# Router's successors in two scaled float16 parts instead of two float32r parts

## Chip, core and metric

The kernel runs on one core of a Trainium2 chip. The metric is device time in microseconds (us). The kernel before took 1172.93 us, the median of three runs (1170.28 to 1175.97).

## The reference, cut to what matters

Three stages follow each other. Attention gives 2304 tokens of 512 features; a router picks one of 8 experts for each token; a dense feed-forward layer follows for all tokens.

```python
attn = softmax(scale * mean_pairs(q) @ k.T)        # (4,8,576,1152), head size 64
x    = (attn @ v)                                  # 2304 tokens x 512
logits = x @ w_gate + modality_bias[modality_id]   # the router
e_idx, gate_w = argmax(logits), softmax(logits)[e_idx]
out[mask] = gate_w[mask] * (relu(x[mask] @ w1[e]) @ w2[e])    # w1: 512x1024, w2: 1024x512
h = out @ w_in                                     # 512x2048
y = (relu(h) + log1p(exp(-abs(h)))) @ w_out        # 2048x512
```

## The kernel before, in words

**Attention** (`attention`, up to about 508 us) keeps q and k in two float16 parts and makes router tables between its heads. The last of these steps stand in `lstage`; step `gb` adds 1e-9 to the softmax sum, `gc` inverts it, and `gd` multiplies the inverse into the scale `r` with which the tokens are written to `x_dram`.

**Experts** (`Moe`, `Early`). Tokens are sorted by expert into blocks of 256. `Early` works on one block while the last router tables are made. Then a loop in `moe_ffn` goes over nine blocks, called block 0 to 8 here. A block has 16 units: eight of `L1` (x @ w1, relu) and eight of `L2` (@ w2). Each unit needs one weight tile `mhl` [128,2,512], which `split` makes out of half of a raw tile `mraw`: ScalarE writes the rounded high part (L645), and VectorE, or GpSimd for splits 7 and 15 of a block, subtracts it to give the low part (L646). A raw tile comes by DMA from the SyncE queue (L633); there are four raw buffers and four `mhl` buffers. In blocks 1 to 7 the same four raw buffers also take 20 tiles of `w_in` and `w_out` (`convert`, L984 to L987: a float64 is turned into a float32), three per block and two in block 7. `split` inside `moe_ffn` (L731, L733) makes high and low parts of these.

Every product is three matmuls (`three`, L608 to L610: high x high, high x low, low x high); the same three stand in `F2` (L779 to L781).

**Feed-forward** (`Ffn`, from about 762 us). `F1` is x @ w_in with the softplus in pieces on ScalarE and VectorE; `F2` is @ w_out, seven units behind. Tokens go in groups of 256 or 512, so a matmul has 256 or 512 columns in `F1` and 512 in `F2`.

The parts are float32r tiles. TensorE and SyncE follow the order of the code in the second half; the order of the other engines is made by the tile framework.

Of the kernel before, what the change touches and what calls it, by code (L numbers as in the profile page):

```python
# [9 lines left out]
F32=mybir.dt.float32; F32R=mybir.dt.float32r; F16=mybir.dt.float16; I32=mybir.dt.int32; U32=mybir.dt.uint32  # L10
ACTF=mybir.ActivationFunctionType; ALU=mybir.AluOpType; AX=mybir.AxisListType
# [5 lines left out]
def attention(ctx,late,tc,I,C,x_dram,LG,gate,fill,early):  # L17

    nc=tc.nc
# [197 lines left out]
    def lstage(b,half,last=False):  # L217

        z={}
# [10 lines left out]
        V=nc.vector  # L230
# [391 lines left out]
class Moe:  # L622
# [16 lines left out]
    def split(s):  # L639
        n=s.nsplit  # L640
        if n>=16: return
        s.nsplit+=1
        t=s.P['hl'].tile([128,2,512],F32R,name="mhl")
        r=s.raw[n//2][:,n%2]
        s.nc.scalar.copy(out=t[:,0],in_=r)  # L645
        (s.nc.gpsimd if n%8==7 else s.nc.vector).tensor_tensor(out=t[:,1],in0=r,in1=t[:,0].bitcast(F32),op=ALU.subtract)  # L646
        s.hl[n]=t
    def advance(s):
        s.split()
# [3 lines left out]
        for _ in range(m): s.split()  # L653
    def T(s,h):
        def f():
            if h==0: s.x=s.P['x'].tile([128,4,2,TB],F32R,name="xx")
            X=s.tr()
            for k in range(4): s.nc.tensor.transpose(X[:,k],s.xg[h][:,128*k:128*k+128],s.K.ident)
            cs=slice(128*h,128*h+128)
            s.nc.scalar.copy(out=s.x[:,:,0,cs],in_=X)  # L660
            s.nc.vector.tensor_tensor(out=s.x[:,:,1,cs],in0=X,in1=s.x[:,:,0,cs].bitcast(F32),op=ALU.subtract)
        return f
    def L1(s,i):
        def f():
            if i==0: s.h=s.P['h'].tile([128,8,2,TB],F32R,name="hT")
            if i%2==0: s.l=s.lt()
            w=s.hl.pop(i)
            for k in range(4):
                s.K.three(s.l[:,i%2],w[:,0,128*k:128*k+128],w[:,1,128*k:128*k+128],(s.x[:,k,0],s.x[:,k,1]),k==0,k==3)
            if i%2:  # L670
                l,z=s.l,slice(i-1,i+1)
                s.nc.scalar.activation(out=s.h[:,z,0],in_=l,func=ACTF.Relu)
                s.nc.vector.scalar_tensor_tensor(out=s.h[:,z,1],in0=l,scalar=0.0,in1=s.h[:,z,0].bitcast(F32),op0=ALU.max,op1=ALU.subtract)
            s.advance()
        return f
    def L2(s,d,half):
# [12 lines left out]
class Early(Moe):  # L689
# [18 lines left out]
        for h in range(2): at(279+3*h,s.T(h))  # L708
    def done(s,d,y):
        yy=s.P['ye'].tile([128,2,TB],F32,name="ye")  # L710
        s.nc.scalar.copy(out=yy,in_=y)
        s.K.lag(2,lambda: s.nc.sync.dma_start(out=s.YE[d//2],in_=yy))
    def step(s,n=1):
        for _ in range(n):
# [2 lines left out]
def moe_ffn(ctx,mst,tc,I,C,Y,YE,wsp,W32,out,convert,ncv,K,P,bl):  # L717
# [3 lines left out]
    nc=tc.nc  # L721
    ident=C['ident']; IDX,IDS,EV,OFF,CIDS=C['IDX'],C['IDS'],C['EV'],C['OFF'],C['CIDS']
    SP=[mybir.EngineType.SP]
    wip=ctx.enter_context(tc.tile_pool(name="wip",bufs=1,reuse_waits="tile"))
    WIH=wip.tile([128,4,DF],F32R,name="WIH"); WOH=wip.tile([128,16,DM],F32R,name="WOH")
    WL=[None]*32
    unit,lag,flush,three,reg=K.unit,K.lag,K.flush,K.three,K.reg
    def split(i):

        h=WIH[:,i%4,512*(i//4):512*(i//4)+512] if i<16 else WOH[:,i-16]  # L730
        nc.scalar.copy(out=h,in_=W32[i])  # L731
        WL[i]=wsp.tile([128,512],F32R,name=f"wl_{i}",tag=f"ws{i}")
        nc.vector.tensor_tensor(out=WL[i],in0=W32[i],in1=h.bitcast(F32),op=ALU.subtract)  # L733
    def WIL(k,f0): return WL[4*(f0//512)+k][:,f0%512:f0%512+128]
    def WOL(fc): return WL[16+fc]
    class Ffn:

        def __init__(s,n,x2,scat,P): s.n=n; s.x2=x2; s.scat=scat; s.P=P; s.g={}; s.m={}; s.e={}; s.hh={}; s.c=4//n; s.nu=16//s.c
        def F1(s,u,ks=range(4)):

            def f():
                q,t=divmod(u,2); c=s.c
                if ks[0]==0:
                    s.hh[u]=(P['pt'].tile([128,4,128],F32,name="tr") if u>=4 and len(ks)==2 else s.P['pl'].tile([128,2,TB],F32,name="l")).rearrange("p a b -> p (a b)").rearrange("p (a b) -> p a b",a=c)
                h=s.hh[u]
                for i in range(c):
                    f0=128*(c*u+i)
                    for k in ks:
                        three(h[:,i],WIH[:,k,f0:f0+128],WIL(k,f0),s.x2(k),k==0 and (i==0 or len(ks)==4),k==3 and (i==c-1 or len(ks)==4))
                if ks[-1]!=3: return  # L750
                if t==0: s.m[q]=s.P['tmp'].tile([128,2,512],F32,name="m"); s.e[q]=s.P['tmp'].tile([128,2,512],F32,name="e")
                hh=h.rearrange("p a b -> p (a b)")
                nc.scalar.activation(out=s.e[q][:,t],in_=hh,func=ACTF.Abs)  # L753
                nc.vector.tensor_scalar(out=s.m[q][:,t],in0=hh,scalar1=0.0,scalar2=None,op0=ALU.max)  # L754
                if t==1:
                    m,e=s.m.pop(q),s.e.pop(q)
                    nc.scalar.activation(out=e,in_=e,func=ACTF.Exp,scale=-1.0)
                    nc.vector.tensor_tensor(out=m,in0=m,in1=e,op=ALU.add)
                    nc.vector.tensor_scalar(out=e,in0=e,scalar1=1.0,scalar2=None,op0=ALU.add)
                    nc.vector.scalar_tensor_tensor(out=m,in0=e,scalar=1.0,in1=m,op0=ALU.subtract,op1=ALU.subtract)  # L760
                    def b():
                        nc.scalar.activation(out=e,in_=e,func=ACTF.Ln)  # L762
                        for i in range(2):
                            nc.vector.tensor_tensor(out=m[:,i],in0=e[:,i],in1=m[:,i],op=ALU.subtract)
                            g=s.P['g'].tile([128,2,512],F32R,name="g"); s.g[2*q+i]=g
                            nc.scalar.copy(out=g[:,0],in_=m[:,i])
                            nc.vector.tensor_tensor(out=g[:,1],in0=m[:,i],in1=g[:,0].bitcast(F32),op=ALU.subtract)
                    lag(BLAG,b)
            return f
        def F2(s,u,ks=None):  # L770
            def f():
                ks_=range(s.n) if ks is None else ks
                if u==0: s.o=[s.P['po'].tile([128,DM],F32,name=f"o{k}") for k in range(s.n)]
                g=s.g[u].rearrange("p s (i w) -> p s i w",i=s.c)
                for i in range(s.c):
                    fc=s.c*u+i
                    for k in ks_:
                        cs=slice(128*k,128*k+128); o=s.o[k]
                        nc.tensor.matmul(o,lhsT=g[:,0,i,cs],rhs=WOH[:,fc],start=(fc==0),stop=False)  # L779
                        nc.tensor.matmul(o,lhsT=g[:,0,i,cs],rhs=WOL(fc),start=False,stop=False)  # L780
                        nc.tensor.matmul(o,lhsT=g[:,1,i,cs],rhs=WOH[:,fc],start=False,stop=(fc==15))  # L781
                if u==s.nu-1:
                    for k in ks_:
                        ob=s.P['io'].tile([128,DM],F32,name="io")
                        if k%2: nc.vector.tensor_copy(out=ob,in_=s.o[k])
                        else: nc.scalar.copy(out=ob,in_=s.o[k])  # L786
                        ap,lim=s.scat(k)
                        nc.gpsimd.indirect_dma_start(out=out,out_offset=bass.IndirectOffsetOnAxis(ap=ap.bitcast(U32),axis=0),in_=ob,in_offset=None,bounds_check=2303,oob_is_err=False)  # L788
            return f
# [5 lines left out]
    XH={}; YR={}; PF=dict(yr=P['raw'])  # L795
# [84 lines left out]
    with tc.For_i(0,nrem,1):  # L880
        with ExitStack() as st:
# [162 lines left out]
```

## Time and profile before

| what | value |
|---|---|
| median of three runs | 1172.93 us |
| the profiled execution's own time | 1169.95 us |
| its span, first to last instruction | 1168.1 us |
| mean granted TensorE clock | 0.997 of full speed |
| TensorE busy (PE) | 1120.9 us, 96%, 7887 instructions |
| weight loads (PEld) | 829.3 us, 71% |
| VectorE (DVE) | 865.9 us, 74% |
| ScalarE (ACT) | 641.3 us, 55% |
| GpSimd (POOL) | 468.5 us, 40% |

A busy TensorE is not one at its peak, since matmuls overlap and their ends are modelled: the pace is read from the distance between the starts of two matmuls. The idle time named in a row is that of the engine before the instruction, with what ended it.

### The profile page before, as it was taken

To read this page: it belongs to the slowest core of one execution; us is meant where nothing else is said; L and a number is where in the kernel's file an instruction comes from. 1 tells how busy PE (TensorE), PEld (TensorE's weight loads), DVE (VectorE), ACT (ScalarE), POOL (GpSimd) and SP (SyncE) were. 2 spreads that over 40 slices of the span, in tenths; PEclk is the share of its full clock that TensorE was granted. 3 is DMA by queue.
4 is the path that set the end of the run, shared out by engine and by line. 5 is a ranking of instruction groups with operands and counts; after the bars stand their busy time and mean duration, and the time that the engine had idled before them with its cause. 6 is when DMAs were issued, how large, how long until landed. Compare 5 with 4: busy or idle time off the path is not lost. (4 is left out here: it accounts for less than half of the span.)

```text
span 1168.1 us, 20814 instructions
## 1 busy us (share of the span) xinstructions
PE 1120.9 (96%) x7887; PEld 829.3 (71%) x7887; DVE 865.9 (74%) x1583; ACT 641.3 (55%) x1096; POOL 468.5 (40%) x512
## 2 busy tenths in 40 slices
PE   5899999999999999999999999999999999999996
PEld 2444555455545555579999999998888888889995
DVE  5778798769876888689798878659667666766662
ACT  5666656766667655647555666555444444444440
POOL 6888877898788866722221121100000100100100
PEclk9999999999999999999999999999999999999998
DMA  9334436341743151436778887531000000000000
GB/s 240 83 83 108 118 89 179 99 118 59 193 115 109 35 145 39 164 94 217 238 249 281 284 272 272 187 90 43 19 1 27 36 5 14 37 5 6 37 10 30
DMA packets 42939, 129.47 MB, mean 111 GB/s; under 512 B 5841, under 2 KB 12881, under 8 KB 40914
## 3 DMA queue, kind: packets, MB, share of 16 engines
q1 hardware_dynamic: 39794, 118.12, 33.9%
q0 software_dynamic: 3040, 9.96, 2.5%
q8 instruction: 65, 1.06, 0.4%
q14 instruction: 40, 0.33, 0.1%
HBM read 108.13 MB, written 20.45 MB: 110 GB/s over the span
## 5 line engine op out<-in xcount | busy, mean ns | idle before, releaser
L121 DVE TENSOR_REDUCE mx<-sr 128x1 f32<-128x384 f32 x432 | 225.4, 549 | 93.0 <-PE sr L117 74.1
L172 ACT ACTIVATE P<-st 128x576 f32<-128x576 f32 x288 | 186.1, 651 | 153.6 <-PE st L169 142.1
L186 POOL TENSOR_TENSOR acc<-P 128x288 f32<-128x288 f32 x192 | 160.2, 856 | 84.4 <-ACT P L172 80.7
L212 PE MATMUL pv<-P,v 128*64 128x288 f32 x1152 | 174.3, 419 | 0.3 <-ACT P L172 0.3
L788 POOL DMA_INDIRECT out_dram<-io,CIDS x18 | 18.7, 1039 | 383.2 <-ACT io L786 335.5
L169 PE MATMUL st<-Q,KB 128*128 128x288 f16 x576 | 153.3, 287 | 2.4 <-ACT Q L152 2.4
L168 PE MATMUL st<-Q,KA 128*128 128x288 f16 x576 | 155.2, 290 | 0.0
L186 POOL TENSOR_TENSOR acc<-acc,P 128x288 f32<-128x288 f32 x176 | 147.7, 860 | 8.5 <-ACT P L172 6.9
L117 PE MATMUL sr<-KA,Q 128*128 128x384 f16 x384 | 113.2, 334 | 17.9 <-DVE mx L121 9.1
L609 PE MATMUL l<-xf,WIH 128*128 128x256 f32 (+1 forms) x384 | 129.1, 336 | 0.1
L608 PE MATMUL l<-xf,WIH 128*128 128x256 f32 (+1 forms) x384 | 129.0, 336 | 0.0
L610 PE MATMUL l<-xf,wl 128*128 128x256 f32 (+1 forms) x384 | 129.0, 336 | 0.0
L645 ACT CAST mhl<-mraw 128x512 fp32r<-128x512 f32 x160 | 97.0, 618 | 54.7 <-PE l L610 22.2
L212 PEld LDWEIGHTS pv<-P,v 128*64 128x64 f32 x1152 | 70.3, 136 | 73.6 <-issue 35.6
L646 DVE TENSOR_TENSOR mhl<-mraw,mhl 128x512 fp32r<-128x512 f32 x140 | 96.3, 707 | 32.9 <-ACT mhl L645 32.4
L168 PEld LDWEIGHTS <-KA 128*128 128x128 f16 x576 | 56.3, 98 | 86.0 <-issue 76.0
L779 PE MATMUL o<-WOH,g 128*128 128x512 f32 x288 | 112.3, 390 | 0.0
L780 PE MATMUL o<-wl,g 128*128 128x512 f32 x288 | 112.2, 390 | 0.0
L781 PE MATMUL o<-WOH,g 128*128 128x512 f32 x288 | 112.0, 389 | 0.0
L762 ACT ACTIVATE e<-e 128x1024 f32<-128x1024 f32 x36 | 38.2, 1060 | 100.3 <-DVE m L760 100.3
L754 DVE TENSOR_SCALAR m<-l 128x512 f32<-128x512 f32 x72 | 49.4, 687 | 57.1 <-ACT e L753 57.0
L94 POOL TENSOR_TENSOR KB<-kr,KA 64x576 f16<-64x576 f32 x64 | 83.6, 1311 | 4.6 <-ACT KA L90 2.4
(260 smaller groups left out, 2543.0 us busy)
## 6 DMA issues: line engine op xcount, KB each, us to landing
mraw<-in_wm_dram SPq DMA_DIRECT2D x80, 512.0 KB, 4.6
kr<-in_k_dram SPq DMA_DIRECT2D x30, 576.0 KB, 9.5
qr<-in_q_dram SPq DMA_DIRECT2D x16, 576.0 KB, 6.5
v<-in_v_dram SPq DMA_DIRECT2D x16, 576.0 KB, 4.4
mraw<-in_w_out_dram SPq DMA_DIRECT2D x16, 512.0 KB, 4.4
stg<-in_w_in_dram SPq DMA_DIRECT2D x12, 512.0 KB, 6.2
y_dram<-w SPq DMA_DIRECT2D x20, 256.0 KB, 4.4
xs_dram<-xs SPq DMA_DIRECT2D x24, 192.0 KB, 2.1
```

Source lines behind the costliest of these rows:

```text
L117: nc.tensor.matmul(sr[:,:KW],lhsT=q[:,h,0,r0:r0+128],rhs=ka[:,h,k0:k0+KW],start=True,stop=True)
L121: nc.vector.tensor_reduce(out=MX[p][:,t,kh:kh+1],in_=sr[:,:KW],axis=AX.X,op=ALU.max,negate=True)
L168: nc.tensor.matmul(st[:,h,:HQ],lhsT=ka[:,h,ks],rhs=q[:,h,0,qs],start=True,stop=False)
L169: nc.tensor.matmul(st[:,h,:HQ],lhsT=kb[:,h,ks],rhs=q[:,h,1,qs],start=False,stop=True)
L172: nc.scalar.activation(out=P[g],in_=ST.pop(g)[:,:,:HQ],func=ACTF.Exp,scale=1.0/16)
L186: for h in range(2): nc.gpsimd.tensor_tensor(out=A[:,h],in0=B_[:,h],in1=P[g][:,h],op=ALU.add)
L212: nc.tensor.matmul(t[64*h:64*h+64,:HQ],lhsT=V[p][:,c,64*h:64*h+64],rhs=P[g][:,h],start=(c==0),stop=(c==NCH-1))
L608: nc.tensor.matmul(o,lhsT=wh_,rhs=x[0],start=first,stop=False)
L609: nc.tensor.matmul(o,lhsT=wh_,rhs=x[1],start=False,stop=False)
L610: nc.tensor.matmul(o,lhsT=wl_,rhs=x[0],start=False,stop=last)
L779: nc.tensor.matmul(o,lhsT=g[:,0,i,cs],rhs=WOH[:,fc],start=(fc==0),stop=False)
L780: nc.tensor.matmul(o,lhsT=g[:,0,i,cs],rhs=WOL(fc),start=False,stop=False)
```

## The change

High and low parts of weights and activations behind the router become float16. Before rounding, weights are scaled by a power of two (SW for the experts, SI and SO for the two feed-forward weights) and tokens by SX, which enters through the router's gate; results are scaled back where PSUM is read. Attention keeps its own order of two chunks and its formats. The edits by kind:

```diff
-            V.tensor_scalar(out=g,in0=g,scalar1=1e-9,scalar2=None,op0=ALU.add)
+            V.tensor_scalar(out=g,in0=g,scalar1=1e-9,scalar2=1.0/SX,op0=ALU.add,op1=ALU.mult)
+SX=16.0; SW=16.0; SI=16.0; SO=256.0
...
-        t=s.P['hl'].tile([128,2,512],F32R,name="mhl")
+        t=s.P['hl'].tile([128,2,512],F16,name="mhl")
         r=s.raw[n//2][:,n%2]
-        s.nc.scalar.copy(out=t[:,0],in_=r)
-        (s.nc.gpsimd if n%8==7 else s.nc.vector).tensor_tensor(out=t[:,1],in0=r,in1=t[:,0].bitcast(F32),op=ALU.subtract)
+        s.nc.scalar.activation(out=t[:,0],in_=r,func=ACTF.Copy,scale=SW)
+        if n%8==7:
+            s.nc.gpsimd.tensor_scalar(out=r,in0=r,scalar1=SW,scalar2=None,op0=ALU.mult)
+            s.nc.gpsimd.tensor_tensor(out=t[:,1],in0=r,in1=t[:,0],op=ALU.subtract)
+        else:
+            s.nc.vector.scalar_tensor_tensor(out=t[:,1],in0=r,scalar=SW,in1=t[:,0],op0=ALU.mult,op1=ALU.subtract)
...
-        s.nc.scalar.copy(out=yy,in_=y)
+        s.nc.scalar.activation(out=yy,in_=y,func=ACTF.Copy,scale=1.0/(SW*SW))
...
-                        if k%2: nc.vector.tensor_copy(out=ob,in_=s.o[k])
-                        else: nc.scalar.copy(out=ob,in_=s.o[k])
+                        if k%2: nc.vector.tensor_scalar(out=ob,in0=s.o[k],scalar1=1.0/SO,scalar2=None,op0=ALU.mult)
+                        else: nc.scalar.activation(out=ob,in_=s.o[k],func=ACTF.Copy,scale=1.0/SO)
```

The same is done to the tiles `x`, `h`, `WIH`, `WOH`, `WL`, `g` and `xf`, to `split` in `moe_ffn`, and to the reads of PSUM in `F1` (Abs with a scale, max with a factor). The code now begins eight lines lower, so L608 to L610 become L611 to L613, L645 becomes L648, and L646 becomes L650 to L653.

On TensorE, at the first unit of a block (l is the result in PSUM, xx the tokens, mhl the weights), before:

```order
L608 MATMUL l_7182<-xx_7059,mhl_7096 128x256
L609 MATMUL l_7182<-xx_7059,mhl_7096 128x256
L610 MATMUL l_7182<-xx_7059,mhl_7096 128x256
L608 MATMUL l_7182<-xx_7059,mhl_7096 128x256
L609 MATMUL l_7182<-xx_7059,mhl_7096 128x256
```

and now:

```order
L611 LDWEIGHTS mhl_7098
L611 MATMUL l_7184<-xx_7061,mhl_7098 128x256
L612 LDWEIGHTS mhl_7098
L612 MATMUL l_7184<-xx_7061,mhl_7098 128x256
L613 LDWEIGHTS mhl_7098
L613 MATMUL l_7184<-xx_7061,mhl_7098 128x256
```

Each float16 matmul has an instruction of its own that loads its weights; a float32r matmul brings them itself. The sequence of products is the same.

On GpSimd, in the block loop (io are gathered tokens, mraw the raw weights), before:

```order
L637 DMA io_7177<-xs_dram_62,IDX_102 128x512
L646 TENSOR_TENSOR mhl_7266<-mraw_7118,mhl_7266 128x512
L637 DMA io_7360<-xs_dram_62,IDX_102 128x512
L637 DMA io_7403<-xs_dram_62,IDX_102 128x512
L646 TENSOR_TENSOR mhl_7420<-mraw_7269,mhl_7420 128x512
```

and now:

```order
L640 DMA io_7179<-xs_dram_62,IDX_102 128x512
L650 TENSOR_SCALAR mraw_7120<-mraw_7120 128x512
L651 TENSOR_TENSOR mhl_7268<-mraw_7120,mhl_7268 128x512
L640 DMA io_7363<-xs_dram_62,IDX_102 128x512
L640 DMA io_7406<-xs_dram_62,IDX_102 128x512
L650 TENSOR_SCALAR mraw_7272<-mraw_7272 128x512
L651 TENSOR_TENSOR mhl_7423<-mraw_7272,mhl_7423 128x512
```

A product with SW, written back into the raw tile, now stands ahead of each subtraction on GpSimd. On VectorE, ScalarE and SyncE no instruction changes its place; only forms and line numbers differ.

## Rows read from the trace of the kernel before

**Rows 1.** Stages, blocks: window us; length, busy PE, PEld, DVE, ACT, POOL; clock; DMA
```profile
508.40:540.70 32.30, 29.41 (x296) 27.99 (x292) 27.70 (x86) 19.75 (x38) 9.35 (x8) 1.00 0.49 158
...
564.70:589.05 24.35, 24.19 (x202) 23.99 (x201) 19.82 (x31) 15.15 (x27) 4.61 (x4) 1.00 0.80 271
589.05:616.20 27.15, 25.82 (x226) 25.08 (x225) 24.78 (x52) 15.07 (x27) 6.12 (x4) 1.00 0.77 256
...
665.20:690.60 25.40, 24.51 (x202) 24.07 (x201) 20.74 (x33) 14.98 (x27) 5.72 (x4) 1.00 0.80 265
...
739.20:762.40 23.20, 23.20 (x196) 23.20 (x195) 11.36 (x17) 12.31 (x24) 2.59 (x2) 1.00 0.50 165
762.40:1158.80 396.40, 396.31 (x2016) 339.08 (x2015) 265.79 (x355) 173.46 (x249) 17.71 (x17) 1.00 0.08 25
```

**Rows 2.** Timeline, TensorE, blocks 6 and 7: start us, us, engine, line, op, tiles
```profile
709.38 0.28 PE L608 MATMUL l<-hT,mhl 128*128 128x256 f32 x1
...
718.26 0.28 PE L610 MATMUL l<-xx,mhl 128*128 128x256 f32 x1
```

**Rows 3.** Timeline, TensorE, the last units of the feed-forward stage
```profile
1140.04 0.39 PE L781 MATMUL o<-WOH,g 128*128 128x512 f32 x1
...
1158.40 0.39 PE L781 MATMUL o<-WOH,g 128*128 128x512 f32 x1
```

**Rows 4.** Timeline, TensorE and its weight loads, float16 matmuls of attention
```profile
305.08 0.29 PE L168 MATMUL st<-Q,KA 128*128 128x288 f16 x1
...
305.57 0.64 PE L117 MATMUL sr<-KA,Q 128*128 128x384 f16 x2
...
305.20 0.10 PEld L168 LDWEIGHTS <-KA 128*128 128x128 f16 x1
```

**Rows 5.** Groups by line and shape: count, then busy us and mean ns, then idle before
```profile
L779 PE MATMUL o<-WOH,g 128*128 128x512 f32 x288 | 112.3, 390 | 0.0
...
L645 ACT CAST mhl<-mraw 128x512 fp32r<-128x512 f32 x160 | 97.0, 618 | 54.7 <-PE l L610 22.2 <-DMA mraw<-in_wm_dram 22.1 <-PE sr L610 4.8
L646 DVE TENSOR_TENSOR mhl<-mraw,mhl 128x512 fp32r<-128x512 f32 x140 | 96.3, 707 | 32.9 <-ACT mhl L645 32.4 <-PE l L610 0.3
...
L608 PE MATMUL l<-hT,mhl 128*128 128x256 f32 x288 | 82.8, 288 | 0.0
...
L608 PE MATMUL l<-xf,WIH 128*128 128x512 f32 x192 | 74.7, 389 | 0.0
...
L608 PE MATMUL l<-xf,WIH 128*128 128x256 f32 x192 | 54.3, 283 | 0.0
...
L90 ACT CAST KA<-kr 128x576 f16<-128x576 f32 x64 | 42.4, 667 | 8.9 <-DMA kr<-in_k_dram 8.3
```

**Rows 6.** One line: count, then duration ns least/median/most, first and last start us
```profile
L86 DVE TENSOR_TENSOR Q<-qs,Q x30: 751/1069/2446, 5.9 to 433.1; 64x576 f16<-64x576 f32 x30
```

**Rows 7.** Timeline of four engines, from block 6 into block 7
```profile
710.07 0.62 ACT L645 CAST mhl<-mraw 128x512 fp32r<-128x512 f32 x1
...
710.77 1.29 POOL L646 TENSOR_TENSOR mhl<-mraw,mhl 128x512 fp32r<-128x512 f32 x1 [1.37 <-ACT mhl L645]
...
712.09 0.33 SPq L633 DMA_DIRECT2D mraw<-in_wm_dram  x1
...
716.25 0.62 ACT L645 CAST mhl<-mraw 128x512 fp32r<-128x512 f32 x1 [1.32 <-DMA mraw<-in_wm_dram]
...
716.90 0.69 DVE L646 TENSOR_TENSOR mhl<-mraw,mhl 128x512 fp32r<-128x512 f32 x1 [0.82 <-ACT mhl L645]
```

**Rows 8.** Groups by line and shape, GpSimd alone
```profile
L64 POOL MEMSET KB<- 64x1152 f16 x2 | 2.1, 1052 | 0.3 <-POOLq L1034 0.3
```

**Rows 9.** Timeline, GpSimd and VectorE, in block 4
```profile
648.45 1.30 POOL L646 TENSOR_TENSOR mhl<-mraw,mhl 128x512 fp32r<-128x512 f32 x1 [11.07 <-ACT mhl L645]
...
649.36 0.93 DVE L646 TENSOR_TENSOR mhl<-mraw,mhl 128x512 fp32r<-128x512 f32 x1 [0.77 <-ACT mhl L645]
```

**Rows 10.** Waits of the SyncE queue from 540 to 762 us: total us, times, longest
```profile
SPq L633 <- DVE w L987: 27.0, 14, 2.4
```

More of the change, by code (lines that the diff above doesn't have):

```diff
@@ L655, in f @@
         def f():
-            if h==0: s.x=s.P['x'].tile([128,4,2,TB],F32R,name="xx")
+            if h==0: s.x=s.P['x'].tile([128,4,2,TB],F16,name="xx")
             X=s.tr()
@@ L660, in f @@
             s.nc.scalar.copy(out=s.x[:,:,0,cs],in_=X)
-            s.nc.vector.tensor_tensor(out=s.x[:,:,1,cs],in0=X,in1=s.x[:,:,0,cs].bitcast(F32),op=ALU.subtract)
+            s.nc.vector.tensor_tensor(out=s.x[:,:,1,cs],in0=X,in1=s.x[:,:,0,cs],op=ALU.subtract)
         return f
@@ L664, in f @@
         def f():
-            if i==0: s.h=s.P['h'].tile([128,8,2,TB],F32R,name="hT")
+            if i==0: s.h=s.P['h'].tile([128,8,2,TB],F16,name="hT")
             if i%2==0: s.l=s.lt()
@@ L672, in f @@
                 s.nc.scalar.activation(out=s.h[:,z,0],in_=l,func=ACTF.Relu)
-                s.nc.vector.scalar_tensor_tensor(out=s.h[:,z,1],in0=l,scalar=0.0,in1=s.h[:,z,0].bitcast(F32),op0=ALU.max,op1=ALU.subtract)
+                s.nc.vector.scalar_tensor_tensor(out=s.h[:,z,1],in0=l,scalar=0.0,in1=s.h[:,z,0],op0=ALU.max,op1=ALU.subtract)
             s.advance()
@@ L724, in moe_ffn @@
     wip=ctx.enter_context(tc.tile_pool(name="wip",bufs=1,reuse_waits="tile"))
-    WIH=wip.tile([128,4,DF],F32R,name="WIH"); WOH=wip.tile([128,16,DM],F32R,name="WOH")
+    WIH=wip.tile([128,4,DF],F16,name="WIH"); WOH=wip.tile([128,16,DM],F16,name="WOH")
     WL=[None]*32
@@ L730, in split @@
         h=WIH[:,i%4,512*(i//4):512*(i//4)+512] if i<16 else WOH[:,i-16]
-        nc.scalar.copy(out=h,in_=W32[i])
-        WL[i]=wsp.tile([128,512],F32R,name=f"wl_{i}",tag=f"ws{i}")
-        nc.vector.tensor_tensor(out=WL[i],in0=W32[i],in1=h.bitcast(F32),op=ALU.subtract)
+        f=SI if i<16 else SO
+        nc.scalar.activation(out=h,in_=W32[i],func=ACTF.Copy,scale=f)
+        WL[i]=wsp.tile([128,512],F16,name=f"wl_{i}",tag=f"ws{i}")
+        nc.vector.scalar_tensor_tensor(out=WL[i],in0=W32[i],scalar=f,in1=h,op0=ALU.mult,op1=ALU.subtract)
     def WIL(k,f0): return WL[4*(f0//512)+k][:,f0%512:f0%512+128]
@@ L752, in f @@
                 hh=h.rearrange("p a b -> p (a b)")
-                nc.scalar.activation(out=s.e[q][:,t],in_=hh,func=ACTF.Abs)
-                nc.vector.tensor_scalar(out=s.m[q][:,t],in0=hh,scalar1=0.0,scalar2=None,op0=ALU.max)
+                nc.scalar.activation(out=s.e[q][:,t],in_=hh,func=ACTF.Abs,scale=1.0/(SX*SI))
+                nc.vector.tensor_scalar(out=s.m[q][:,t],in0=hh,scalar1=0.0,scalar2=1.0/(SX*SI),op0=ALU.max,op1=ALU.mult)
                 if t==1:
@@ L764, in b @@
                             nc.vector.tensor_tensor(out=m[:,i],in0=e[:,i],in1=m[:,i],op=ALU.subtract)
-                            g=s.P['g'].tile([128,2,512],F32R,name="g"); s.g[2*q+i]=g
+                            g=s.P['g'].tile([128,2,512],F16,name="g"); s.g[2*q+i]=g
                             nc.scalar.copy(out=g[:,0],in_=m[:,i])
-                            nc.vector.tensor_tensor(out=g[:,1],in0=m[:,i],in1=g[:,0].bitcast(F32),op=ALU.subtract)
+                            nc.vector.tensor_tensor(out=g[:,1],in0=m[:,i],in1=g[:,0],op=ALU.subtract)
                     lag(BLAG,b)
@@ L806, in xs @@
         w=RW[j][1]
-        if j not in XH: XH[j]=PF['x'][j%len(PF['x'])].tile([128,4,2,512],F32R,name="xf")[:,:,:,:w]
+        if j not in XH: XH[j]=PF['x'][j%len(PF['x'])].tile([128,4,2,512],F16,name="xf")[:,:,:,:w]
         t=XH[j][:,k]; y=YR.pop((j,k)); hi,lo=t[:,0],t[:,1]
         nc.scalar.copy(out=hi,in_=y)
-        nc.vector.tensor_tensor(out=lo,in0=y,in1=hi.bitcast(F32),op=ALU.subtract)
+        nc.vector.tensor_tensor(out=lo,in0=y,in1=hi,op=ALU.subtract)
     def todone(j):
@@ L814, in done @@
             w=bl[j].nd; z=slice(d%2+1-w,d%2+1); yy=P['ye'].tile([128,2,TB],F32,name="ye")[:,:w]
-            nc.scalar.copy(out=yy,in_=y[:,:w])
+            nc.scalar.activation(out=yy,in_=y[:,:w],func=ACTF.Copy,scale=1.0/(SW*SW))
             def st():
@@ L887, in done @@
             def done(d,y):
-                if d==1: z['x2']=P['x'].tile([128,4,2,TB],F32R,name="xx")
+                if d==1: z['x2']=P['x'].tile([128,4,2,TB],F16,name="xx")
                 w=slice(d-1,d+1)
-                nc.scalar.copy(out=z['x2'][:,w,0],in_=y)
-                nc.vector.tensor_tensor(out=z['x2'][:,w,1],in0=y,in1=z['x2'][:,w,0].bitcast(F32),op=ALU.subtract)
+                nc.scalar.activation(out=z["x2"][:,w,0],in_=y,func=ACTF.Copy,scale=1.0/(SW*SW))
+                nc.vector.scalar_tensor_tensor(out=z['x2'][:,w,1],in0=y,scalar=1.0/(SW*SW),in1=z['x2'][:,w,0],op0=ALU.mult,op1=ALU.subtract)
             b.done=done
```

## The prediction

> **What bounds the kernel now.** I read the busy times by stage first [rows 1], since the whole-span shares mix three stages. In the feed-forward stage TensorE is busy for 396.31 of 396.40 us, with VectorE at 67% and ScalarE at 44%: that stage is TensorE's pace and nothing else. In the expert blocks TensorE is also nearly full, but a block lasts from 23.20 us (block 8, which fetches no weights for a next block) to 27.15 us (block 2, which also makes the compaction table); blocks 3 to 7 lie between 24.1 and 25.4. A block has 192 matmuls. So the reader should see two kinds of block: 0 and 8, paced by TensorE, and 1 to 7, which already run late by some tenths to 1.6 us.
>
> Second come the distances between matmul starts. In the expert stage 74 matmuls of 256 columns lie between 709.38 and 718.26 us [rows 2]: 120.0 ns each. At the clock granted there (1.00, the 2.4 GHz level [rows 1]) 256 columns stream in 106.7 ns, so 13.3 ns are lost per matmul. With 512 columns 81 matmuls lie between 1140.04 and 1158.40 [rows 3]: 226.7 ns against 213.3, again 13.3 lost. Float16 matmuls of 288 columns in attention start 0.49 us apart in four steps [rows 4]: 122.5 ns against 120.0, 2.5 lost. The loss does not grow with the columns, so it belongs to the instruction.
>
> **The sum: TensorE's pace.** Each of the 3936 matmuls behind the router changes form. I take 13.3 - 2.5 = 10.8 ns saved per matmul; reading the float16 steps to 0.01 us leaves 8.3 to 13.3.
> Feed-forward: three lines each of 192 + 192 and 288 matmuls [rows 5], 2016 in all, as the window counts [rows 1]. 2016 x 10.8 ns = 21.8 us. All of it is on the path, as TensorE never waits there and the other engines have a third of their time free. Behind the last matmul at 1158.40 [rows 3] 9.7 us remain to the span's end, untouched.
> Expert blocks: 9 x 192 = 1728 matmuls, 18.7 us at most, 2.08 per block.
> Early block: 192 matmuls, 2.1 us at most, in a window of 32.3 us where 192 x 120 ns is 23 us [rows 1]; the rest waits for router tables. I take a third, 0.7 us; 0 and 2.1 are its ends.
>
> **The sum: what the other engines pay.** A float32 subtract becomes a subtract with a factor, mixing float32 and float16. The nearest mixed row is attention's subtract to float16: at best 751 ns for 576 columns [rows 6], where the float32r one takes 707 ns on average for 512 [rows 5]; 0 more is what I take. Its median of 1069 ns is a stretch with GpSimd at work, priced below, and bounds it at 1.5 times from above. On ScalarE the scaled copy to float16 has a near row in the cast of 576 columns, 667 ns, against 618 for 512 [rows 5]: 1.2 ns a column, which carries 618 to 695; again 0. Both are hidden wherever TensorE sets the pace. The router's extra factor rides in an instruction that was there. Read-outs of PSUM change form only.
>
> The one new instruction is the product on GpSimd: two per block, ahead of splits 7 and 15. No row shows it. From below, a fill of 1152 columns takes 1052 ns [rows 8], so 512 columns take 0.47 us; from above, the subtract with two inputs takes 1.29 us [rows 7]. It reads one stream and writes one, which lies between; I take 0.8, nearer the fill.
>
> Its place matters. At the end of a block that converts weights, the second raw load of the next block waits for split 15 [rows 7]: ScalarE's cast starts at 710.07, GpSimd ends at 710.77 + 1.29 = 712.06, the load is issued at 712.09 and lands when the next cast starts, at 716.25; VectorE ends at 716.90 + 0.69 = 717.59, and the matmul that needs it starts at 718.26 [rows 2], 0.67 later. Split 15 starts once the unit before 709.38 has freed its buffer, so TensorE has 74 matmuls to cover this chain: 8.88 us now, 74 x 109.2 ns = 8.08 us after. The chain takes 717.59 - 709.38 = 8.21 us now and 9.0 with the product. TensorE then waits about 0.9 us (0.6 to 1.4 with the ends of the price). That happens at six block ends, since blocks 1 to 6 convert three tiles.
>
> So 2.08 - 0.9, some 1.15 us, is the most that such a block gains. Nor will it get all: the four raw buffers take 11 fills in such a block; the SyncE queue stands waiting for one to be freed, 27.0 us in total behind converts alone [rows 10], and fill, casts and converts do not get faster. VectorE already has 19.82 of 24.35 us in block 1 [rows 1], and 2.08 us less makes that over 89%. I count a third, 0.4 us for each of blocks 1 to 7, 2.8 in all (ends: -1 and +1.15 each), and the full 2.08 for blocks 0 and 8, 4.2. Blocks: 7.0 us.
>
> Total: 21.8 + 0.7 + 7.0 = 29.5 us. From the profiled execution's own 1169.95 us this gives 1140.4. The median shown is 3.0 us above that execution, so I predict 1143.5 us.
>
> A rule to weigh is in the Trainium skill, SBUF — State Buffer, section Who interferes with whom: a VectorE instruction with two inputs in SBUF and a GpSimd instruction that reads SBUF exclude each other. The trace agrees: while GpSimd's subtract ran from 648.45 to 649.75, VectorE's, begun at 649.36, took 0.93 us [rows 9] where 0.69 is usual [rows 7]. By this rule the new product holds up VectorE as well, some 0.25 us to 0.8 us per split, which is the rival below.
>
> **Rivals.** (a) The fills keep up and every block runs at TensorE's pace: 42.6 us saved less what the product can't hide. For it: the waits of blocks 3 to 7 are short today. Against it: the chain above has only 0.67 us in hand. Time: 1172.9 - 41.5 = 1131.4.
>
> (b) GpSimd and VectorE give the blocks' gain back. With 0.8 us more per split GpSimd works 4.2 us per block on splits instead of 2.6; if VectorE is held up for each, the late splits meet converts in its queue, which runs in order, and each of blocks 2 to 7 loses 1 us against now. Then 21.8 + 0.7 + 4.2 - 6 = 20.7, and with 1 us lost in block 0 and 1 too, 19: 1153.5 us. For it: the 0.93 us row and VectorE's share. Against it: 15 of 16 splits are still paced by TensorE's release of their buffers.
>
> (c) The 13.3 ns belong to something other than the number format (tile layout, three products on one PSUM tile). Then nothing is saved and the product costs a little: 1174. Against it: the loss is the same at 256 and 512 columns and in two stages.
>
> (d) Slower: the weight load that is now an instruction of its own is not hidden. In these matmuls the load is 0.10 us [rows 4]. Added in full to 109.2 and 215.8 ns it gives 209 and 316: 89 ns more than now for each of 3936, +350 us, 1523 us. It decides as soon as more than 10.8 ns of a load shows. Against it: in attention the load at 305.20 lies under the matmul before it, and the distance stays at 122.5 ns [rows 4]; with 256 columns 106.7 ns still cover 98 to 100. The Trainium skill, TensorE: Matmul & The Clock Gate, section Packing small matmuls — row/col tiling, speaks for (d): a load overlaps a running matmul only if it goes to other rows of the array. The trace does not agree, as these loads fill all 128 rows and overlap.
>
> **How the numbers follow.** Forecast 0.55, (a) 0.17, (b) 0.20, (c) 0.05, (d) 0.03. The forecast's own range is 1138 to 1149. The range that should hold 8 in 10 goes to 1132 below, where part of (a) stays out, and to 1156 above, past (b). About 0.5%, 5.9 us, is what can be told from no change: faster 0.92, within 0.05 (c), slower 0.03 (d).
>
> **What would show it.** Matmul distances of 109 ns (256 columns) and 216 ns (512) show the price per matmul; 374.6 us for the feed-forward window shows the first term; blocks 0 and 8 near 21.9 and 21.1 us and blocks 1 to 7 near 24 show the second; a GpSimd product near 0.8 us and TensorE waiting for a VectorE split in the first units of a block show the third. If those blocks take 22 us the raw buffers never bound them, and if 512-column matmuls stay at 226 ns the argument falls whole.

## The result and the profile after

The changed kernel took 1150.99 us (median of four runs, 1149.02 to 1156.94) against 1172.18 us for the kernel before: a ratio of 0.9829, 95% interval 0.9808 to 0.985. That is 21 us faster; 29.5 were forecast. The profiled execution took 1149.53 us with a span of 1147.7 us, against 1169.95 and 1168.1 us. The time lies inside the stated range of 1132 to 1156 us, 2 us above the forecast's own range (1138 to 1149) and nearest to rival (b), 1153.5 us.

The stages first, set against [rows 1]. The windows are Early, blocks 0, 1, 5 and 8 and the feed-forward stage; the columns are as there.

```profile
507.82:540.87 33.05, 27.41 (x297) 23.10 (x294) 27.23 (x86) 20.11 (x38) 13.35 (x10) 1.00 0.45 147
540.87:564.75 23.88, 22.33 (x201) 19.45 (x200) 21.26 (x42) 14.12 (x25) 9.87 (x6) 1.00 0.62 194
564.75:588.91 24.16, 22.50 (x203) 19.41 (x201) 18.43 (x30) 14.44 (x26) 7.89 (x6) 1.00 0.81 287
...
666.14:691.17 25.03, 22.57 (x203) 19.32 (x201) 20.14 (x33) 15.06 (x27) 8.27 (x6) 1.00 0.80 269
...
740.43:761.51 21.08, 21.08 (x195) 18.70 (x193) 10.95 (x17) 12.04 (x23) 5.29 (x4) 1.00 0.52 176
761.51:1138.47 376.96, 374.57 (x2018) 197.09 (x2015) 263.42 (x355) 172.61 (x249) 20.17 (x17) 1.00 0.08 27
```

The reader is to see that the gain stands in one row. The feed-forward stage went from 396.40 to 376.96 us. Block 8 went from 23.20 to 21.08 us, full TensorE as before. Blocks 0 to 7 together and Early did not get shorter; only TensorE's share in them fell, from 24.19 of 24.35 us in block 1 to 22.50 of 24.16. Measured from the first matmul of block 0 to the first of the feed-forward stage, the nine blocks took 221.5 us before and 220.6 us after.

The distances between matmul starts, in the timeline of TensorE in block 8 and near the end of the feed-forward stage, to set against [rows 2, 3]:

```profile
751.13 0.27 PE L612 MATMUL l<-hT,mhl 128*128 128x256 f16 x1
...
759.98 0.27 PE L612 MATMUL l<-hT,mhl 128*128 128x256 f16 x1
...
1118.66 0.38 PE L789 MATMUL o<-WOH,g 128*128 128x512 f16 x1
...
1138.09 0.38 PE L789 MATMUL o<-WOH,g 128*128 128x512 f16 x1
```

Between the first two rows lie 81 matmuls: 109.2 ns each. Between the last two lie 90: 215.9 ns each. Both are the forecast's numbers.

Where the gain of the blocks went is read from TensorE's waits from 540 to 762 us (total us, times, longest). After:

```profile
PE l L612 <- DVE hT L680: 6.4, 7, 1.0
PE l L613 <- DVE mhl L653: 6.1, 7, 1.3
PE cix L577 <- DVE co L569: 2.6, 3, 1.3
PE l L613 <- POOL mhl L651: 1.8, 3, 0.9
PE l L611 <- ACT ye L718: 0.9, 1, 0.9
```

and before:

```profile
PE l L608 <- ACT ye L711: 1.5, 1, 1.5
PE l L609 <- DVE hT L673: 1.2, 3, 0.7
PE cix L577 <- DVE co L569: 1.1, 2, 1.0
PE l L610 <- DVE mhl L646: 0.9, 2, 0.6
```

The listed waits rose from 4.7 to 17.8 us, by 13.1 us. At 120.0 and 109.2 ns the 1728 matmuls alone take 207.4 and 188.7 us, 18.7 us less, and the blocks took 0.9 us less, so the gain that was lost is 17.8 us; the rest of it lies in waits too short or too scattered for this list. The waits for VectorE's low parts (of the weights, `mhl`, and of the activations, `hT`) rose from 2.1 to 12.5 us. A faster TensorE met work that did not come sooner.

One such place is the middle of block 4. The timelines of VectorE and TensorE after:

```profile
652.25 0.43 DVE L993 TENSOR_SCALAR w<-mraw 128x512 int32<-128x512 int32 x1 [2.41 <-DMA mraw<-in_w_out_dram]
652.72 0.69 DVE L994 SCALAR_TENSOR_TENSOR w<-mraw,w 128x512 int32<-128x512 int32 x1
653.32 0.68 DVE L680 SCALAR_TENSOR_TENSOR hT<-l,hT 128x512 f16<-128x512 f32 x1
653.92 0.68 DVE L995 SCALAR_TENSOR_TENSOR w<-mraw,w 128x512 int32<-128x512 int32 x1
654.52 0.69 DVE L653 SCALAR_TENSOR_TENSOR mhl<-mraw,mhl 128x512 f16<-128x512 f32 x1
...
655.27 0.28 PE L613 MATMUL l<-hT,mhl 128*128 128x256 f16 x1 [0.87 <-DVE mhl L653]
```

and the same instruction of VectorE before:

```profile
650.58 0.43 DVE L985 TENSOR_SCALAR w<-mraw 128x512 int32<-128x512 int32 x1 [0.29 <-DMA mraw<-in_w_out_dram]
```

VectorE runs these instructions in the order of the program, the same as before. The first operation of a convert waits for its tile to land, 2.41 us where it waited 0.29 before, and the low parts that TensorE needs stand behind it. The matmul at 655.27 pays for it. Over all blocks VectorE's waits for tiles to convert rose from 8.3 to 15.4 us.

GpSimd's two instructions for split 7 of the same block, and TensorE's matmuls around the one that needs it:

```profile
648.38 1.49 POOL L650 TENSOR_SCALAR mraw<-mraw 128x512 f32<-128x512 f32 x1 [9.31 <-DMA mraw<-in_wm_dram]
649.95 1.16 POOL L651 TENSOR_TENSOR mhl<-mraw,mhl 128x512 f16<-128x512 f32 x1
...
651.01 0.27 PE L612 MATMUL l<-xx,mhl 128*128 128x256 f16 x1
651.17 0.28 PE L613 MATMUL l<-xx,mhl 128*128 128x256 f16 x1
```

The product took 1.49 us, not 0.8. It ends the slack: the low part is there at 651.11 and the matmul starts at 651.17, 0.05 us later than its distance of 0.11 would have had it. In 18 of the 20 splits on GpSimd the matmul starts within 0.1 us of its end; before, 1.88 us lay between the two in most of them.

The groups by line and shape, after, for the splits (to set against [rows 5, 7]):

```profile
L648 ACT ACTIVATE mhl<-mraw 128x512 f16<-128x512 f32 x160 | 98.1, 625 | 45.3 <-DMA mraw<-in_wm_dram 22.2 <-PE l L613 15.5 <-PE sr L613 4.3
L653 DVE SCALAR_TENSOR_TENSOR mhl<-mraw,mhl 128x512 f16<-128x512 f32 x140 | 95.7, 703 | 27.3 <-ACT mhl L648 26.5 <-PE l L613 0.3
...
L650 POOL TENSOR_SCALAR mraw<-mraw 128x512 f32<-128x512 f32 x20 | 31.1, 1554 | 100.6 <-ACT mhl L648 65.9 <-DMA mraw<-in_wm_dram 18.6 <-DVE mhl L653 8.4
L651 POOL TENSOR_TENSOR mhl<-mraw,mhl 128x512 f16<-128x512 f32 x20 | 24.8, 1240 | 1.7
```

The casts (625 ns for 618) and VectorE's subtracts (703 for 707) cost what they did, as taken. So on average VectorE's subtracts were not held up by the product.

### The profile page after: what moved, and what is told of

Same layout as the page of the kernel before. It is cut to its first block, busy times and chain, and to the rows that moved or that the text cites. A ratio compares the mean times of both kernels' runs of the same rounds, so it can differ in the third digit from the quotient of the medians.

```text
span 1147.7 us, 20868 instructions
## 1 busy us (share of the span) xinstructions
PE 1082.5 (94%) x7887; PEld 641.0 (56%) x7887; DVE 865.6 (75%) x1583; ACT 641.2 (56%) x1096; POOL 504.9 (44%) x532
## 5 line engine op out<-in xcount | busy, mean ns | idle before, releaser
L796 POOL DMA_INDIRECT out_dram<-io,CIDS x18 | 21.1, 1174 | 359.1 <-ACT io L794 312.7
L611 PE MATMUL l<-xf,WIH 128*128 128x256 f16 (+1 forms) x384 | 125.1, 326 | 1.0 <-ACT xf L817 1.0
L612 PE MATMUL l<-xf,WIH 128*128 128x256 f16 (+1 forms) x384 | 125.1, 326 | 0.2 <-DVE xf L818 0.2
L613 PE MATMUL l<-xf,wl 128*128 128x256 f16 (+1 forms) x384 | 125.1, 326 | 0.0
L648 ACT ACTIVATE mhl<-mraw 128x512 f16<-128x512 f32 x160 | 98.1, 625 | 45.3 <-DMA mraw<-in_wm_dram 22.2
L653 DVE SCALAR_TENSOR_TENSOR mhl<-mraw,mhl 128x512 f16<-128x512 f32 x140 | 95.7, 703 | 27.3 <-ACT mhl L648 26.5
L787 PE MATMUL o<-WOH,g 128*128 128x512 f16 x288 | 109.1, 379 | 1.2 <-ACT io L794 0.8
L788 PE MATMUL o<-wl,g 128*128 128x512 f16 x288 | 109.1, 379 | 0.0
L789 PE MATMUL o<-WOH,g 128*128 128x512 f16 x288 | 109.1, 379 | 0.0
L612 PE MATMUL l<-hT,mhl 128*128 128x256 f16 x288 | 78.5, 272 | 6.4 <-DVE hT L680 6.4
```

The costliest lines, as they stand in the source:

```text
L611: nc.tensor.matmul(o,lhsT=wh_,rhs=x[0],start=first,stop=False)
L612: nc.tensor.matmul(o,lhsT=wh_,rhs=x[1],start=False,stop=False)
L613: nc.tensor.matmul(o,lhsT=wl_,rhs=x[0],start=False,stop=last)
```

## The experiments

Each ratio is to runs of the kernel before on the same chip. "Blocks" is the time from the first matmul of block 0 to the first of the feed-forward stage in the profiled execution. The last column counts matmuls of 256 columns in the expert stage that start 0.21 us apart instead of 0.11 (see the run with six raw buffers). Counts of 3 to 5 are not the slower pace described there: those matmuls still take 0.27 to 0.28 us each, as in the rest of the stage, where the slow ones take 0.42. A profile is one execution of each run, and executions of one kernel differ by 3 to 12 us, so the ratios, which use all of them, say what an edit is worth, and the blocks say where one execution spent it.

| run | us | before | ratio, 95% interval | blocks, us | at 0.21 us |
|---|---|---|---|---|---|
| the change | 1150.99 | 1172.18 | 0.9829, 0.9808-0.985 | 220.6 | 5 |
| e1_no_product | 1151.02 | 1174.47 | 0.9796, 0.9773-0.9819 | 219.6 | 4 |
| e2_f32r_product | 1180.91 | 1174.47 | 1.0052, 1.0037-1.0066 | 227.6 | - |
| e3_raw6 | 1163.17 | 1174.47 | 0.9901, 0.9878-0.9925 | 233.7 | 75 |
| e5_no_product_raw6 | 1157.02 | 1174.47 | 0.984, 0.9818-0.9863 | 230.1 | 16 |
| f1_no_converts | 1137.22 | 1171.8 | 0.9711, 0.9688-0.9735 | 206.3 | 19 |
| f2_one_op_converts | 1148.89 | 1171.8 | 0.9818, 0.9793-0.9843 | 218.0 | 3 |
| f4_spread_converts | 1150.3 | 1171.8 | 0.9821, 0.9797-0.9844 | 224.2 | 54 |
| h2_hl6 | 1155.53 | 1171.8 | 0.9862, 0.9831-0.9894 | 229.0 | 59 |
| g6_transfer_only | 1143.6 | 1173.29 | 0.9744, 0.9719-0.9769 | 217.4 | 18 |
| g7_late_bits | 1151.49 | 1173.29 | 0.9816, 0.9773-0.9859 | 224.2 | 54 |
| g8_late_bits_raw6 | 1153.13 | 1173.29 | 0.9834, 0.9804-0.9863 | 222.2 | 46 |
| k1_converts_early | 1169.59 | 1173.04 | 0.9971, 0.9954-0.9989 | 228.1 | 59 |

**The product taken away.**

```diff
-SX=16.0; SW=16.0; SI=16.0; SO=256.0
+SX=16.0; SW=1.0; SI=16.0; SO=256.0
...
-            s.nc.gpsimd.tensor_scalar(out=r,in0=r,scalar1=SW,scalar2=None,op0=ALU.mult)
```

> The changed kernel with SW = 1 instead of 16 and without GpSimd's product ahead of splits 7 and 15; all else as in the changed kernel. Theory G (the product on GpSimd, measured at 1.49 us and not the 0.8 us forecast, took the gain of the expert blocks, directly as TensorE's wait for splits 7 and 15 and by freeing the raw tile later): the waits at these splits go, blocks 1 to 7 fall from 24-25.9 us to about 23-23.5, the time is 1143 to 1146 us. Theory R (the four raw buffers and their refill bind the blocks at about 24 us whatever GpSimd does): blocks 1 to 7 stay between 23.8 and 25.4, the time is 1149 to 1151 us.

Its windows for blocks 0 and 1, and two rows of TensorE's waits from 540 to 762 us:

```profile
541.94:563.77 21.83, 21.83 (x201) 19.65 (x201) 20.64 (x41) 14.11 (x25) 6.30 (x4) 1.00 0.60 195
563.77:589.06 25.29, 22.70 (x203) 19.40 (x201) 18.05 (x30) 14.47 (x27) 4.89 (x4) 1.00 0.82 280
```

```profile
PE l L613 <- DVE mhl L652: 7.5, 14, 1.3
PE l L612 <- DVE hT L679: 5.9, 6, 1.0
```

Block 0, which makes no converts, falls from 23.88 to 21.83 us: there the product took the whole gain. The other runs without it bear this out where the matmuls of block 0 keep their pace (22.14, 22.18 and 22.28 us); in six more, 12 to 25 of these matmuls run at the slower pace and the block takes 23.2 to 24.6 us. Blocks 1 to 7 stay (176.8 us for the seven, 175.7 with the product), and TensorE's waits for VectorE stay at 13.4 us. Only their places change: the wait in the first unit of blocks 5 and 6 goes, and one at unit 9 (counted from 0) comes in blocks 3, 5, 6 and 7. Theory G holds for block 0 and Early (32.34 us for 33.04), but its time, 1143 to 1146 us, missed; theory R holds for the blocks with converts. The ratio is lower than that of the change, but the intervals overlap.

**The product alone, in float32r.**

```diff
+        if n%8==7: s.nc.gpsimd.tensor_scalar(out=r,in0=r,scalar1=1.0,scalar2=None,op0=ALU.mult)
```

> The kernel before (float32r parts) with the product alone added: GpSimd multiplies the raw tile by 1.0 in place ahead of splits 7 and 15. Theory G: at float32r's pace the low part of these splits had 1.88 us in hand, so TensorE does not wait for it, but the raw tile is freed 1.5 us later; the six block ends have 0.67 us in hand, which costs 0.6 to 0.9 us each: 1176 to 1179 us. Theory R (the product only fills slack): 1172 to 1174 us.

It costs 0.52%, 6.1 us, and the blocks take 6.1 us more than before. Theory R is out; theory G has the sign, but its range ended at 1179 us, and 1180.9 were measured. TensorE's listed waits for the low parts from GpSimd are 0.2 us there, its waits for `hT` rise from 1.2 to 4.1 us, and SyncE's waits for GpSimd to free a raw tile from 23.4 to 50.7 us. So at float32r's pace the product acts for the most part by what comes later behind it, the raw tile among it. But it left its own result little room: in 6 of the 20 splits the matmul starts within 0.06 us of GpSimd's end, where theory G counted on 1.88 us in hand. The listed waits grew by about 3 us; how the rest of the 6.1 us divides is not shown.

**Six raw buffers**, with and without the product.

```diff
-[('raw','mraw',4,0),('hl','mhl',4,0),
+[('raw','mraw',6,0),('hl','mhl',4,0),
```

> The changed kernel with six raw buffers instead of four in the expert stage. Theory G: loads no longer wait for splits 7 and 15, but TensorE still waits for their low parts, 0.1 to 0.6 us twice per block: the converts come earlier, the waits for the low part of hT go, 1144 to 1148 us. Theory R: the refill was the bound, so blocks 1 to 7 fall to 22 us: 1135 to 1141 us. If neither holds (VectorE or the DMA rate bind), 1149 to 1151 us.

> Both edits: SW = 1, no product on GpSimd, and six raw buffers. Theory G: about what the run without the product alone gives, 1141 to 1145 us. Theory R: TensorE's pace in all blocks, 1131 to 1137 us, and most of it is already there with six raw buffers alone.

Both theories missed: both runs are slower, by 12 and 6 us (the first by about 8 us going by the ratios, since the change was timed on another chip). Two things in the first run's trace. The timelines of GpSimd and TensorE at the end of block 1:

```profile
587.25 3.40 POOL L650 TENSOR_SCALAR mraw<-mraw 128x512 f32<-128x512 f32 x1
590.74 1.19 POOL L651 TENSOR_TENSOR mhl<-mraw,mhl 128x512 f16<-128x512 f32 x1
...
591.98 0.28 PE L613 MATMUL l<-hT,mhl 128*128 128x256 f16 x1 [2.61 <-POOL mhl L651]
...
593.21 0.42 PE L611 MATMUL l<-xx,mhl 128*128 128x256 f16 x1
593.42 0.42 PE L612 MATMUL l<-xx,mhl 128*128 128x256 f16 x1
```

and the windows of the wait, of the next 0.7 us and of the 3.1 us behind them (the eighth column is the clock):

```profile
589.10:591.98 2.88, 0.27 (x4) 0.01 (x1) 1.72 (x3) 0.77 (x2) 2.74 (x2) 1.00 0.85 283
592.10:592.80 0.70, 0.70 (x8) 0.63 (x7) 0.00 (x0) 0.07 (x1) 0.00 (x0) 1.00 1.01 380
592.90:596.00 3.10, 3.10 (x18) 2.21 (x16) 1.39 (x2) 1.57 (x3) 0.00 (x0) 0.51 0.99 382
```

With more buffers the framework sets most converts earlier in VectorE's order, by one to three subtracts. VectorE works almost without a pause while the product runs, and the product takes 3.40 us here and at three more block ends. TensorE stands for 2.6 us, and 0.9 us after it has begun again its granted clock falls to 0.51, the 1.2 GHz level: matmuls start 0.21 us apart for 3.2 us. That happens five times in this run. 75 matmuls at 0.104 us more are 7.8 of the 13.1 us by which the blocks got longer. The run without the product has only 16 such matmuls; why its blocks too got 10.5 us longer than with four buffers stays open: the converts moved there in the same way, but no run shows what that alone costs.

**What the converts hold.** Three runs, on the kernel without the product: no converts in the blocks; the transfer and VectorE's first operation; the transfer alone.

```diff
-                for z in convert(ncv,P['raw'],"mraw"): z()
+                nc.vector.memset(W32[ncv],0.0)                                             # none
+                for z in convert(ncv,P['raw'],"mraw")[:2]: z()                             # one operation
+                nc.vector.memset(W32[ncv],0.0); convert(ncv,P['raw'],"mraw")[0]()          # transfer
```

> The run without the product (SW = 1), and the 20 converts of w_in and w_out left out of the expert blocks: no transfer, no raw tile, no bit operations on VectorE; a fill with zero takes their place and moves into attention. The two feed-forward weights are then wrong from tile 12 on. Theory C (what holds blocks 1 to 7 at 24 to 25 us, before the change and after, are the converts): blocks 0 and 1 and 3 to 7 take 21.8 us like block 0 of the run without the product, block 2 about 24, the expert stage gets 20 us shorter: 1125 to 1130 us. Theory S (the splits themselves, cast, subtract and expert weight loads, bind): blocks 1 to 7 stay above 24: over 1143 us.

> The run without the product, and of each convert in the expert blocks only the transfer and the first, short VectorE operation (0.43 us) kept; two of 0.6 us left out, so the low bits and the sign of these weights are missing. If VectorE's work binds: blocks 1 to 7 fall to 22-22.5 us, 1128 to 1134 us. If the transfer and the four raw buffers bind: blocks 1 to 7 stay at 24 to 25, 1143 to 1151 us.

> The run without the product (SW = 1), and of each convert in the expert blocks only the transfer into a raw tile kept: VectorE does nothing with it (a fill with zero in attention takes its place, so the feed-forward weights are wrong from tile 12 on). Theory V (VectorE works in order and stands waiting for the converted tile to land, 17 us in all, while low parts that TensorE needs stand behind it): the expert stage, 219.6 us with whole converts and 206.3 without any, falls to 206-209; 1136 to 1139 us. Theory T (the transfers themselves and the raw buffers they take hold up the expert weights): it stays at 215-219; 1144 to 1149 us.

The window of the nine blocks with whole converts, without any, with one operation and with the transfer alone, one row from each run:

```profile
541.94:761.50 219.56, 201.94 (x1816) 175.04 (x1816) 174.53 (x297) 130.92 (x236) 40.47 (x32) 1.00 0.75 252
```

```profile
542.69:749.02 206.33, 200.54 (x1816) 176.66 (x1816) 144.38 (x239) 129.82 (x236) 40.73 (x32) 0.99 0.67 217
```

```profile
541.28:759.30 218.02, 203.35 (x1816) 174.08 (x1816) 147.96 (x260) 127.72 (x236) 39.75 (x32) 1.00 0.76 253
```

```profile
541.27:758.67 217.40, 202.70 (x1816) 175.39 (x1816) 142.03 (x240) 128.51 (x236) 39.65 (x32) 0.99 0.77 254
```

Theory C has the cause but not the size. Without converts the blocks lose 13 us, and TensorE's waits for VectorE in them fall from 13.4 to 3.4 us. Blocks 3 and 6 take 21.83 us, TensorE's pace; but the stage was to lose 20 us and the time to be 1125 to 1130, and it is 1137.22. Blocks 0 and 1 did not fall: 15 matmuls of block 0 run at the slower pace, and block 1, still with the splits of `w_in` and `w_out` in VectorE's queue, takes 26.33 us. Blocks 1 and 3 of this run:

```profile
566.30:592.63 26.33, 22.75 (x203) 19.24 (x200) 24.75 (x38) 14.34 (x26) 6.68 (x4) 1.00 0.62 212
616.44:638.27 21.83, 21.83 (x202) 19.66 (x200) 13.67 (x20) 13.50 (x24) 4.33 (x4) 1.00 0.73 235
```

The other two runs came out on the transfers' side: 1148.89 us, and 1143.6 us with a stage of 217.4, 0.4 us below that side's range of times. Two of VectorE's three operations are worth 1.5 us in the blocks and nothing by the ratio, though they are 27 of its 175 busy us. The transfer alone keeps 11 of the 13 us in the profiled executions. The ratios, which use all executions, say less: against the run without the product the transfer-only run gains about 6 us (give or take 4), of about 10 that the run without converts gains. So VectorE's wait for the tile is worth some part of the gain too, and how the two divide is not settled: the transfer holds between 4 of 10 and 11 of 13 us. In the transfer-only run TensorE's waits for VectorE are down to 5.4 us. What is late then are the raw weights themselves: TensorE waits 8.4 us for ScalarE's cast (1.0 with whole converts), the cast for the landing of the weights, and SyncE's next load for the landing of the tile that holds the buffer. SyncE's row shows the raw buffer at work; whether the rate of the transfers adds to it is not shown. ScalarE's wait with the transfer alone, SyncE's in the same run, and ScalarE's with whole converts:

```profile
ACT mhl L648 <- DMA mraw<-in_wm_dram: 56.9, 26, 5.4
```

```profile
SPq L636 <- DMA mraw<-in_w_out_dram: 24.3, 11, 5.4
```

```profile
ACT mhl L648 <- DMA mraw<-in_wm_dram: 20.6, 14, 4.2
```

**Ways round it.** All on the kernel without the product: the converts spread over blocks 1 to 8; six buffers for the split weights; VectorE's operations some units behind the transfer, with four and with six raw buffers; 12 of the 20 converts moved into attention.

```diff
-            if j>=1 and ncv<32 and n in CVN:                                   # spread
+            if j>=1 and ncv<32 and n in (CVN if j%2 else CVN[:2] if j==8 else CVN[::2]):
-[('raw','mraw',4,0),('hl','mhl',4,0),                                          # hl6
+[('raw','mraw',4,0),('hl','mhl',6,0),
-                for z in convert(ncv,P['raw'],"mraw"): z()                     # late bits (3; 4 with raw6)
+                a,*v=convert(ncv,P['raw'],"mraw"); a(); lag(3,lambda v=v: [z() for z in v])
-CH=((2,1),(3,1),(6,1),(7,1),(10,1),(11,1),(14,6))                              # early, with CVN=(2,)
+CH=((2,3),(3,3),(6,3),(7,3),(10,3),(11,3),(14,6))
```

> The run without the product, and the 20 converts spread over blocks 1 to 8: three in odd blocks, two in even ones (before: three in blocks 1 to 6, two in block 7, none in 8). Theory C: blocks 4 and 6 about 1 us shorter (2 too), block 7 a little longer, block 8 from 21.0 to 22 us: 1145 to 1149 us. Otherwise within 1.5 us of the run without the product.

> The run without the product, and six buffers instead of four for the split weights (mhl; float16 has freed the space). Splits may then run two units further ahead of TensorE. If TensorE's release of these buffers paces the late splits: the 7.5 us of waits for VectorE's low parts go, 1140 to 1145 us. If raw tiles or converts bind: within 2 us of the run without the product, 1148 to 1153 us.

> The run without the product, and VectorE's three bit operations of a convert put three units (4 us) behind its transfer in the code; four raw buffers. Theory V: VectorE's wait for landing goes, 1143 to 1147 us. Theory T: a raw buffer is held longer, so loads come later: 1150 to 1156 us.

> The run without the product, the bit operations four units behind their transfer, and six raw buffers. Theory V: neither VectorE nor the buffers wait, and blocks 1 to 7 fall to 22.5-24 us: 1136 to 1144 us. Theory T (transfers bind by their rate): 1148 to 1158 us, as with six raw buffers without the shift.

> The run without the product (SW = 1), and 12 of the 20 converts moved out of the expert blocks into attention (24 there instead of 12, three instead of one for six of its heads); one is left in each of blocks 1 to 8. Nothing is left out. Theory T (the converts' transfers through the raw buffers hold blocks 1 to 7 at 24 to 25 us): these blocks fall to 22-23 us and the expert stage from 219.6 to 207-211 us; attention has VectorE at 77% and pays 0 to 8 us for 12 more converts of 1.7 us each: 1135 to 1147 us. Otherwise the stage stays above 215 and the time is 1149 us or more.

None gains on the run without the product. Spreading (1150.3 us) and the two late-operation runs (1151.49 and 1153.13) came as the side that expected nothing had it; six `mhl` buffers (1155.53) came above both of its ranges, and moving the converts early (1169.59) far above the hoped-for 1135 to 1147. All five have 46 to 59 matmuls 0.21 us apart, 4.8 to 6.1 us, and each gets another order of VectorE's instructions from the framework with its edit, so none is a clean test of its one idea. The last one is clear in one respect. Attention pays 14 us (523.83 us up to Early's first matmul for 509.60), and a block with one convert still takes 24 us. Its VectorE and TensorE in block 5:

```profile
695.89 0.43 DVE L992 TENSOR_SCALAR w<-mraw 128x512 int32<-128x512 int32 x1 [1.80 <-DMA mraw<-in_w_out_dram]
...
698.16 1.29 DVE L652 SCALAR_TENSOR_TENSOR mhl<-mraw,mhl 128x512 f16<-128x512 f32 x2
...
698.90 0.28 PE L613 MATMUL l<-hT,mhl 128*128 128x256 f16 x1 [0.53 <-DVE mhl L652]
700.71 0.27 PE L612 MATMUL l<-hT,mhl 128*128 128x256 f16 x1 [0.99 <-DVE hT L679]
```

Here one convert is enough to delay the low part of split 9 and the next `hT` in VectorE's queue, and TensorE loses 1.8 us at these two matmuls. The reading that fits these runs is that there are two holds: VectorE's wait in order, and the raw buffer that the transfer takes. It is argued and not shown apart: how much each costs alone in the changed kernel stays open, since the order of VectorE's instructions changed with every edit that removed one.

## Why the prediction was right, and where not

**Distances**: right, 109.2 and 215.9 ns for 109.2 and 215.8. Rivals (c) and (d) are out.

**Feed-forward, 21.8 us forecast, 19.6 came**: TensorE's busy time in the window is 374.57 us, the forecast 374.6. The window is 2.4 us longer than that, since TensorE now waits a little where it never did ("TensorE never waits there" no longer held): at the stage's start and behind the first group of tokens, where a PSUM tile must be read out first. One of these waits in the timeline of TensorE:

```profile
826.42 0.38 PE L787 MATMUL o<-WOH,g 128*128 128x512 f16 x1 [0.78 <-ACT io L794]
```

**Block 8, 2.08 us**: right (23.20 to 21.08). **Early, 0.7 us**: it got 0.7 us longer; without the product it took the 32.3 us that it took before, and the gain did not come either. TensorE waits 3.2 us in Early for gathered tokens, where it waited 0.6 before and waits 1.4 without the product; what makes the gather late is not shown.

**The product, 0.8 us, 0.9 us per block end**: this step failed in size and in place. The range given, 0.47 to 1.29, left the measured 1.49 us outside: the bound from above, the subtract with two inputs, was none. And only the chain through the raw tile was priced. A wait at the start of a block did come, 1.5 us in each of blocks 4 to 6 (gaps of 1.60 us between matmul starts) and 0.4 in blocks 2 and 3. But it is not the product's alone: without the product it is still 1.4 us in block 4, and where it went a wait at unit 9 came. And with 1.49 us the low part itself also became late at splits 7 and 15 of every block, block 0 too, where the full 2.08 us were counted and 0.13 came.

**Blocks 1 to 7, 2.8 us**: they got 1.2 us longer (174.4 to 175.7 us by first matmuls). This is the largest part of the miss, 4.0 of some 9 us. The forecast's reason, that raw buffers and converts run at their own pace, was right, and the third of the gain that was still counted was a guess and was not there. It does not come when the product goes either.

**Rival (b)** named VectorE's queue, converts ahead of late splits, and its time, 1153.5 (1154.2 by its own terms), is nearest. Its cause was GpSimd holding VectorE up; the run without the product shows the same 13 us of waits for VectorE, and the run without converts 3.4, so the cause is in the main the converts, and that its time came near is luck. **Rival (a)**, 1131.4 us, is out of reach as long as the converts stand in the blocks: even without them the time is 1137 us.

The stated range held because it was drawn past rival (b); the forecast itself, 29.5 us for the 21.2 measured, was right in its first term and in block 8, and counted gains in Early and blocks 0 to 7 that did not come.

So the sum over the profiled executions, before less after: feed-forward 19.6 (396.18 to 376.58 by matmul starts), block 8 2.0, block 0 0.1, blocks 1 to 7 -1.2, Early -0.7, attention and the tail 0.7: 20.4 us of span.

## What to carry to other kernels

Price a faster engine stage by stage, and take the gain only where that engine was full and what feeds it has room: here the feed-forward stage gave nine tenths of it, and the blocks that convert weights, which looked up to 99% full of TensorE, gave none, since the converts, by VectorE's queue and the raw buffers, held them at about the same length. Before counting on an instruction that is added to an engine off the path, ask how much slack its result has at the consumer, not only what buffer it frees. More buffers are no safe cure where a scheduler sets the order: here they moved converts ahead of other work in VectorE's queue, and the kernel got slower. And before a trace is used to share out a gain, set its execution against the spread of all runs.

## What the runs showed of the hardware that was not expected

- GpSimd's float32 product of one input, in place, takes 1.49 us at least for 512 columns, more than its subtract of two inputs into float16 at 1.16 us. In the run with six raw buffers four of 20 took 3.40 us, each while VectorE ran subtracts and bit operations of two inputs with hardly a pause. A busy VectorE is not enough for this: at 616.75 us of the same run, and in others, the product took 1.49 us with VectorE busy throughout, and VectorE's operation of two inputs took 1.11 us where 0.68 is usual. So either of the two engines can be the one that is held; the prediction counted on VectorE alone.
- In the run with six raw buffers TensorE's granted clock fell to half for some 3 us after each of five waits of 2.3 to 2.6 us, 0.1 to 1.4 us after it had begun again; waits of 0.9 to 1.1 us in that run were not followed by it. Other runs do not fit so simply. It fell after two waits of 0.94 and 0.99 us that lay 1.8 us apart in the run with converts moved early (596.09 us), and did not after the same two waits in the run without the product (580.22 us); nor did it after one of 3.2 us in Early of the changed kernel, or of 2.5 and 2.8 us ahead of block 0 in the runs without the product and with one operation. What decides is not shown.
